# Gated mix of two attention branches: q and k weights loaded in column groups, heads at a stride of 32 floats in PSUM, later small loads, another order of all work

## The chip, the cores and the metric

One core of a Trainium2 chip. The metric is the time of one execution on the device in microseconds (us). Five in-order queues carry the program: PE (matrix multiplies, with its weight loads shown as PEld), ACT, DVE and POOL (elementwise engines), and SP, which here issues nearly all DMAs.

## The reference

The input x is 2048 tokens of 640 values. Both branches have 32 heads of 20 values, and a sigmoid gate per token mixes them.

```python
g = sigmoid((x * gate_w).sum(-1))
# branch A: linear attention, per head, feature map of 2 x 20
phi(q) = [softmax(q @ w_phi), softmax(-q @ w_phi)]        # and phi(k) alike
a = (phi(q) @ (phi(k).T @ v)) / (phi(q) @ phi(k).sum(0)) @ wo_A
# branch B: four segments of 512 tokens, per head
p     = softmax(q @ k.T * scale + causal_mask)            # inside the segment
a_dot = p @ v
a_mem = (elu1(q) @ M) / (elu1(q) @ z)                     # M, z from the segments before
o     = sigmoid(beta) * a_mem + (1 - sigmoid(beta)) * a_dot
M    += elu1(k).T @ v;   z += elu1(k).sum(0)
b = o @ wo_B
out = g * a + (1 - g) * b
```

## The kernel before

Everything is bfloat16 in on-chip memory with float32 sums in PSUM. Channels lie on partitions in five chunks of 128 (NCH = 5). For branch B, four heads share a chunk at offsets of 32 partitions: heads 0 to 19 take 20 of each 32 (the main part, 400 columns of the weights), and the 240 columns of the other 12 heads fill the 12 rows left in each block (the spare part). The weights of q and k are first loaded as they are (tiles stq and stk) and then copied into this image, WB, main and spare part apart (L606 and L607, called WB copies).

The work of branch B runs over four segments and, in each, eight groups of heads: matmuls of q with k (L754, called QK here) into PSUM, exp on ACT (L763, tiles expT, and ej for two of the groups), the causal mask on POOL (L767), and the product with the values v1B (L795, called PV), whose result oU is written to DRAM (opk) and read back as rows by head (oP) and as the row sums (dc). The reciprocals of the sums (L820) go out through rxB and come back spread over the rows (rrB), and L835 multiplies. b_mem accumulates M over the segments (L716, L719, and the masked product Mz, L721), b_out makes the memory part (Nmm on PE, then L864 to L869 into mo) and transposes it by DMA (moT).

Branch A makes the keys' features (E, with the norm at L909 on DVE or POOL), adds them up over all tokens, closes the sums with one column-sum matmul over all token tiles (a_fin, L962, called the column sum here), and then, per segment, makes the queries' features ET (L1008), their normalizer (rx, rr, L1040), the product U with the key-value sums (L1055), the reciprocal of the denominators (L1060) and the scaled result oA (L1064), which a DMA transposes (oTA). The last step (final, L1083 and L1084) multiplies oTA and oP by the output weights and adds both in PSUM; one copy to out and one DMA per token tile ends it.

The program builds one list of operations with dependencies. What runs where and when is written out: ORDER lists all operations in base 36 in the order in which they are given to their queues, CHOICE says for each eviction of PSUM whether ACT or DVE does it (L606 is the ACT form, L607 the DVE form, of the helper evac) and for each norm of E whether DVE or POOL does it, and WHERE names the buffer of each tile. An engine never passes a waiting instruction. spin is a matmul with no use, which keeps PE busy in the first microseconds.

Of the kernel before, what the change touches and what calls it, by code (L numbers as in the profile page):

```python
# [7 lines left out]
ALU = mybir.AluOpType  # L8
# [5 lines left out]
D = 640  # L14
H = 32
# [19 lines left out]
2t 3y 2r 3z 40 15 6v 34 7p 7w 3e 21 28 7x 22 23 35 3f 2w 26 27 2x 7q 29 24 2a 7m 6w 41 42 3g 25 43 7r 7n 45 2b 44 6y 2g 2h 30 4d 46 4f 32 4e 2c 2d 33  # L35
4g p3 p4 31 3h p5 p8 2 p9 6x c 49 4b 3i of e og 4a 3k 3j 2y 6z 2z 1r 3l on 3n 3m 2k oh 70 oo ok 39 op 1s oy 1t 2i 3o 3p 2l 2j 37 72 17 36 7i 2e 4h 1f
4c oz 2f 38 7j 47 4l pa 7k 16 4m 3b 48 4n 4o 3d 7l os ov ow 4p ox ot 4r ou 4i dc 4j 3c ol 4q 4s 8q dd 3a om p6 p7 4u 4v 4t oi pq 4w 4x pr ps 19 oq p0
oj 54 4y p1 55 or p2 80 50 ph 56 51 52 r4 81 4z 57 f 58 7u pe pi r5 pj pg 5c 53 59 pf 7v 7y 5d 5e 5l 5m 5n pk pl 10o 5a pb 7z 5g pc 85 pd 83 pv 5i 5o
3q 8a 18 5h 5v 8u 8b 8c 5f 5x qh 10p 5r 1u 73 pm qi 5w pn 74 4k dk 5s dl 5j 5k 5p 5t 6m 6n pw q1 q6 8t 6o q7 q8 5b q2 10q 5u 5y 5z 60 5q 61 6c 6e da
10r 6d po 67 di pp 71 68 84 db py c0 bw px 6f bz 69 63 dj pz 6p q0 pt 6a 6b 82 6q qb 64 r1 65 pu q3 qc 6i q4 6k r2 by qe q5 qs 75 76 6j bx 6l qf qg q9  # L40
dq qj qd 6r qa r3 8w c1 77 8d 66 8x 8y 88 dr dg qk 6s 8e 8f ql dh 90 91 92 c2 qt c4 do dp qu 1o 93 qm qo 6g 95 6h 96 94 97 ds qn 86 qp qv dt qw c3 qr
8z 9f 9g qq 98 8g qx sk qy 9h c5 c6 8h 9i 8i 9b r6 9c r9 9d 1e 87 rk 3 qz ho ra r0 sl rh sm hq r7 8j rb ri rj 8r rp 9j 8v rl 9e 89 8k 8l rm 99 6t rq
hr 9k r8 8s rr 9n 9o rs 9p 9l de rt df hp 9a rn hs s3 9w e2 9x rc 9y dm e3 ro e4 9r rd sf j8 ru dn rv 9s sg re rf rw rg s4 s5 62 e5 9q 9t j9 dv ht a6
s6 hu e6 s0 s7 a7 3r a8 hw e7 1c rx a2 s1 s2 sp 9z a9 sn s8 a4 sc ry a3 rz dx 9u 9v aa sq s9 so a0 a5 sd 7a se a1 ae j6 af ab j7 an ag ap ao j2 9m ac
# [39 lines left out]
def d_mm(*ns):  # L84
    return sum(max(n / 2400.0 + 0.004, 0.034) for n in ns)
# [222 lines left out]

class GatedMix(Graph):
# [167 lines left out]
    def setup(self):  # L477
# [695 lines left out]
```

## Time and profile before

| what | value |
|---|---|
| time, median of 3 runs | 329.12 us (329.91, 327.7, 329.12) |
| profiled execution | 332.06 us |
| span in its trace | 330.3 us (1.76 us lie around it) |
| busy in the span | PE 289.1 us (88%), ACT 247.8 (75%), DVE 234.9 (71%), POOL 124.6 (38%) |
| instructions | PE 2883, DVE 392, ACT 324, POOL 136 |
| DMA | 37.38 MB, mean 113 GB/s |
| granted PE clock over the span | 0.948 of full |

Busy shares are means over stages that have different limits: a share of 88% can be one stage at 99% and another with holes. The profiled execution is 2.94 us above the median of the three runs, and all sums over rows are made against it.

### The profile page before, as it was taken

What the parts mean: (1) busy time and instruction counts of PE and PEld (TensorE: products, weight loads), DVE (VectorE), ACT (ScalarE), POOL (GpSimd) and SP (SyncE); (2) the same over time, 40 slices, a digit from 0 to 9 for tenths busy, and PEclk for the clock granted to TensorE, in tenths of its full rate; (3) what the DMA queues carried; (4) which work ended last, traced back from release to release, by engine and by line L of the source; (5) the groups of instructions that cost most, each with busy time, mean ns of one, the idle gap of its engine ahead of it and who ended that gap; (6) DMA issues with size and microseconds to landing.
All of it is one profiled execution on the core that took longest, in us unless ns stands there. A gap on an engine that the chain in (4) does not pass through costs nothing.

```text
span 330.3 us, 7013 instructions
## 1 busy us (share of the span) xinstructions
PE 289.1 (88%) x2883; PEld 149.0 (45%) x2883; DVE 234.9 (71%) x392; ACT 247.8 (75%) x324; POOL 124.6 (38%) x136
## 2 busy tenths in 40 slices
PE   1899999999999969998899869997999668879695
PEld 1345554544545535445354444433444223446443
DVE  1444696989989999999998577565823736868740
ACT  4458889799887969897998729999897996941002
POOL 3321418238476546739342211244332373430000
PEclk9999999999999999999999999999999955579979
DMA  6992675050541441601506556661192263897933
GB/s 188 286 207 48 175 97 128 2 128 2 91 36 37 97 63 15 182 2 30 170 17 197 158 84 158 144 152 35 32 189 43 69 210 63 217 204 182 182 86 119
DMA packets 72271, 37.38 MB, mean 113 GB/s; under 512 B 55184, under 2 KB 69168, under 8 KB 72240
## 3 DMA queue, kind: packets, MB, share of 16 engines
q1 hardware_dynamic: 71488, 36.08, 47.8%
q10 hardware_dynamic: 656, 0.82, 0.7%
q8 instruction: 23, 0.38, 0.5%
q0 software_dynamic: 96, 0.04, 0.2%
q14 instruction: 8, 0.07, 0.1%
HBM read 14.01 MB, written 12.10 MB: 79 GB/s over the span
## 4 chain that ended last, share of the span: by engine, by line
PE 41%; DVE 21%; DMA 16%; ACT 11%; SPq 7%; issue 3%; POOL 0%; DVEq 0%
PE ps L627 9%; PE ps L1083 9%; ACT expT L763 7%; PE ps L1003 5%; DVE acc L949 4%; SPq L472 4%; PE ps L754 4%; SPq L468 3%; PE ps L795 3%; DMA dc<-opk 3%; DVE z L907 3%; PE ps L894 2%; DMA opk<-oU 2%; PE ps L1084 2%; DMA rrB<-rxB 2%
## 5 line engine op out<-in xcount | busy, mean ns | idle before, releaser
L763 ACT ACTIVATE expT<-ps 128x1024 bf16<-128x1024 f32 x128 | 124.5, 1030 | 20.8 <-PE ps L754 19.8
L767 POOL TENSOR_SCALAR_AFFINE_SELECT expT<-expT 128x512 bf16<-128x512 bf16 x96 | 72.4, 761 | 120.5 <-ACT expT L763 108.5
L627 PE MATMUL ps<-xT,WB 128*128 128x512 bf16 x200 | 50.6, 390 | 1.9 <-DVE oU L607 1.0
L763 ACT ACTIVATE ej<-ps 128x1024 bf16<-128x1024 f32 x32 | 31.2, 1040 | 3.0 <-PE ps L754 2.9
L909 POOL TENSOR_TENSOR E<-E,z 128x1280 bf16<-128x1280 bf16 x11 | 28.0, 2548 | 10.4 <-DVE z L908 9.4
L767 POOL TENSOR_SCALAR_AFFINE_SELECT ej<-ej 128x1024 bf16<-128x1024 bf16 x16 | 19.2, 1197 | 31.2 <-ACT ej L763 31.2
L1083 PE MATMUL ps<-Wo,oTA 128*128 128x512 bf16 x80 | 24.8, 395 | 5.5 <-DVE oP L877 4.7
L754 PE MATMUL ps<-qkm 20*128 20x512 bf16 (+3 forms) x320 | 21.7, 322 | 8.5 <-DVE oU L607 2.0
L627 PEld LDWEIGHTS ps<-xT,WB 128*128 128x128 bf16 x200 | 17.9, 100 | 23.9 <-issue 4.9
L949 DVE TENSOR_TENSOR acc<-acc,E 64x1280 bf16<-64x1280 bf16 x31 | 27.8, 896 | 1.2 <-DMA acc<-acc 0.3
L795 PE MATMUL ps<-expT,v1B 128*21 128x384 bf16 (+2 forms) x384 | 26.1, 342 | 2.6 <-POOL ej L767 1.2
L1008 ACT ACTIVATE ET<-ps 128x512 bf16<-128x512 f32 x40 | 22.5, 637 | 7.1 <-PE ps L1003 6.7
L606 ACT ACTIVATE out<-ps 128x640 bf16<-128x640 f32 x9 | 6.2, 703 | 28.6 <-PE ps L1084 22.8
L607 DVE CAST oU<-ps 128x512 bf16<-128x512 f32 x26 | 17.7, 682 | 10.3 <-PE ps L795 10.2
L907 DVE TENSOR_REDUCE z<-E 128x64 f32<-128x1280 bf16 x16 | 23.6, 1476 | 1.5 <-ACT E L901 1.4
L649 PE MATMUL ps<-WvB,xT 128*128 128x512 bf16 x80 | 23.9, 381 | 0.6 <-DVE M L716 0.5
L901 ACT ACTIVATE E<-ps 128x640 bf16<-128x640 f32 x32 | 22.1, 706 | 3.0 <-PE ps L895 2.5
L894 PE MATMUL ps<-WvA,xT 128*128 128x512 bf16 x80 | 23.6, 380 | 0.9 <-DVE qkm L607 0.5
L1003 PE MATMUL ps<-xT,WqA 128*128 128x512 bf16 x100 | 23.7, 380 | 0.5 <-DVE oA L1064 0.5
L894 PE MATMUL ps<-WkA,xT 128*128 128x512 bf16 x80 | 23.4, 380 | 0.5 <-DVE KVZacc L937 0.5
L1083 PE MATMUL ps<-Wo,oP 128*128 128x512 bf16 x80 | 23.8, 383 | 0.0
L607 DVE CAST qkm<-ps 128x512 bf16<-128x512 f32 x24 | 16.2, 683 | 8.0 <-PE ps L627 7.9
(130 smaller groups left out, 549.4 us busy)
## 6 DMA issues: line engine op xcount, KB each, us to landing
opk<-oU SPq DMA_DIRECT2D x16, 256.0 KB
oP<-opk SPq DMA_DIRECT2D x4, 640.0 KB
rx<-rc SPq DMA_DIRECT2D x16, 160.0 KB
rr<-rx SPq DMA_DIRECT2D x4, 640.0 KB
out_dram<-out SPq DMA_DIRECT2D x16, 160.0 KB
scr<-qkm SPq DMA_DIRECT2D x16, 120.0 KB
qks<-scr SPq DMA_DIRECT2D x16, 120.0 KB
stq<-in_B_wq_dram ACTq DMA_DIRECT2D x1, 800.0 KB, 5.2
```

Source lines behind the costliest of these rows:

```text
L607: return e.tensor_copy(o(), i())
L627: r = e.matmul(self.pf(pt, 0, 0, LSEG), lhsT=self.WB[:, w, kc, 128 * c:128 * (c + 1)], rhs=xT[:, kc, LSEG * n:LSEG * (n + 1)], start=(kc = ...
L754: r = e.matmul(self.pf(pts[i // 2], i % 2, c0, N), lhsT=view(32 * i, 32 * i + DH, 1, 128 * j, 128 * (j + 1)), rhs=view(32 * i, 32 * i + DH ...
L763: self.op("act", d_act(1024), lambda e, p=p, o=o: e.activation(o(), self.pbanks(pts[p], 0, 2, 512), ACT.Exp, scale=scale), W=[(pts[p], 0), ...
L767: self.op("pool", d_pool(n_el), lambda e: e.affine_select(view(), view(), pattern=pat, compare_op=ALU.is_ge, fill=0.0, base=0, channel_mul ...
L795: r = e.matmul(self.ps[32 * i:32 * i + 21, 512 * ad.t[0] + 128 * j:512 * ad.t[0] + LSEG], lhsT=vt[:, j, h, :], rhs=src[:, i, c0:c0 + N], s ...
L894: e.matmul(self.pf(pt, 0, 0, 512), lhsT=l, rhs=W[:, kc, 0:512], start=(kc == 0), stop=(kc == 4))
L907: self.op("dve", 1.48, lambda e: e.tensor_reduce(z[:, :], Ev(), axis=AX.X, op=ALU.add), R=[(E, 0), (E, 1)], W=[(z, "*")], claim=[rz], pr=p ...
L909: self.op(("dve", "pool"), {"pool": d_pool(1280, 2), "dve": 1.56}, lambda e: e.tensor_tensor(Ev(), Ev(), rz[:, :].rearrange("p (h o) -> p ...
L949: self.op("dve", 0.9, lambda e, src=src: e.tensor_tensor(acc[lo:lo + 64, :], acc[lo:lo + 64, :], src(), ALU.add), R=[(self.Et[t], 0), (sel ...
L1003: r = e.matmul(self.pf(pt, 0, 0, LSEG), lhsT=self.WqA[:, kc, 128 * c:128 * (c + 1)], rhs=xT[:, kc, LSEG * S:LSEG * (S + 1)], start=(kc == ...
L1083: e.matmul(self.pf(pt, 0, 0, 512), lhsT=l, rhs=self.Wo[:, c, 0:512], start=(c == 0), stop=(c == 9))
```

## The change

The loads of B's q and k weights, one DMA each before (stq on ACT's queue, stk on SP's behind the third part of xtok), become eight DMAs on SP: for the column groups (0,2) and (2,5) of the chunks, q and k, main and spare part. The copies into WB go by group, and a projection waits for the copies of its own group alone. The three loads on POOL's queue (gw, beta, wphi) wait for the first group of k. In PSUM, the tiles of Nmm and U have a head every 32 floats (ph) where they had a head every 21 in two banks, so the reciprocal, the product of mo and that of oA are one instruction of 640 columns where they were two of 320. There are 17 spins where there were 5, and they read the identity only. ORDER, CHOICE and WHERE are new.

```diff
-NSPIN = 5
+NSPIN = 17
 ORDER = """
-5 6 4 0 8 1h 1g 11 1i 7 1 k m o 1j s i q 14 r 9 l d 12 13 1k j a p n 2u 1l h 2v 1m 2m 2n b 1n 2o 2p 2s g 3u v 6u 7s 7o 3v 3w 2q t u x 10 y w 3x z 7t
+0 1 106 107 108 109 17 10a 10b 5 s t 7 6 4 8 1n 9 c 1o d w a 1p b f 1u e j x u 10c 1m g q 10d 1t h 10e 10f v r 2w 30 1s 1r 11 1q 3c 3d 2x m 38 39 1w
...
-CHOICE = "000110011010001011111111100111010100111111010000110111110001101111110011011101000111111111011010000100111111001111001111100111110011010001010001111010111100001000"
+CHOICE = "1111100011000101110011111100000101001111101001011001110111100110101110010111111010011110101101101110100000110111001011110101011110110111011111000111100001111100000100"
...
+CGRP = ((0, 2), (2, NCH))
...
+    def ph(self, t, h0, n, e=21):
+        return self.ps[:, 512 * t.t[0] + 32 * h0:512 * t.t[0] + 32 * (h0 + n)].rearrange("p (h e) -> p h e", e=32)[:, :, 0:e]
...
-        stq = self.dma("act", self.stq[:, :, :], wsrc(ins["B_wq"]), W=[(self.stq, "*")], pr=-50, name="stq", issue=0.45, lat=6.2)
-        stk = self.dma("sp", self.stk[:, :, :], wsrc(ins["B_wk"]), W=[(self.stk, "*")], pr=-50, name="stk", issue=0.5, lat=5.0, after=ld[2:3])
...
+        for gi, (c0, c1) in enumerate(CGRP):
+            for w, (st, name) in enumerate(((self.stq, "B_wq"), (self.stk, "B_wk"))):
+                src = wsrc(ins[name])
+                for z, (a0, a1) in enumerate(((80 * c0, 80 * c1), (400 + 48 * c0, 400 + 48 * c1))):
+                    stk = self.dma("sp", st[:, :, a0:a1], src[:, :, a0:a1], W=[(st, (z, gi))], pr=-50 + gi, name="s" + "AB"[gi] + "ms"[z], issue=0.5, lat=5.0)
+                    if gi == 0:
+                        ska = stk
...
-                self.op("pe", d_mm(*[512] * 5), mm, R=[(self.WB, (w, z, k0)) for z in range(2) for k0 in (0, 2)] + self.xr(n), W=[(pt, 0), (qk, (w, c))], pr=pr, name="qkproj")
+                self.op("pe", d_mm(*[512] * 5), mm, R=[(self.WB, (w, z, int(c >= CGRP[0][1]), k0)) for z, k0 in ((0, 0), (0, 3), (1, 0))] + self.xr(n), W=[(pt, 0), (qk, (w, c))], pr=pr, name="qkproj")
...
-            for f in range(2):
-                self.op("dve", d_dve(320, 1, True), lambda e, f=f, pt=pt, sm=sm, t=t, oA=oA: e.scalar_tensor_tensor(
...
+            self.op("dve", d_dve(640, 1, True), lambda e, pt=pt, sm=sm, t=t, oA=oA: e.scalar_tensor_tensor(
+                out=oA[:, :].rearrange("p (h d) -> p h d", d=DH), in0=self.ph(pt, 0, H, 32)[:, :, 0:DH],
+                scalar=self.g[:, t:t + 1], in1=sm[:, :].rearrange("p (h o) -> p h o", o=1).to_broadcast([128, H, DH]), op0=ALU.mult, op1=ALU.mult),
...
-            return e.matmul(self.pf(pt, 0, 0, 512), lhsT=self.ident[:, :], rhs=self.xT[:, 0, 0:512], start=True, stop=True)
+            return e.matmul(self.pf(pt, 0, 0, 512), lhsT=self.ident[:, :], rhs=self.ident[:, :].rearrange("p (o c) -> p o c", o=1).to_broadcast([128, 4, 128]), start=True, stop=True)
```

Over the whole program DVE goes from 392 to 362 instructions, ACT from 324 to 327, POOL from 136 to 138, and SP issues 181 DMAs where it issued 174. Three places where the order differs:

SP's queue at the start, before. xtok is the first 512 tokens, xT the transposed input of segment 1, WvB the values' weights, wkT a transposed weight of branch A.

```order
L472 DMA xtok<-in_A_x_dram 128x640 x4
L472 DMA stk<-in_B_wk_dram 128x5x640
L468 DMA_TRANSPOSE xT<-in_A_x_dram 128x5x512
L472 DMA WvB<-in_B_wv_dram 128x5x640
L468 DMA_TRANSPOSE wkT<-in_A_wqkv_dram 128x5x640
L468 DMA_TRANSPOSE wqT<-in_A_wqkv_dram 128x5x640
```

The same place after:

```order
L478 DMA xtok<-in_A_x_dram 128x640 x4
L478 DMA stq<-in_B_wq_dram 128x5x160
L478 DMA stq<-in_B_wq_dram 128x5x96
L478 DMA stq<-in_B_wq_dram 128x5x240
L478 DMA stq<-in_B_wq_dram 128x5x144
L478 DMA stk<-in_B_wk_dram 128x5x160
L478 DMA stk<-in_B_wk_dram 128x5x96
L478 DMA stk<-in_B_wk_dram 128x5x144
L478 DMA stk<-in_B_wk_dram 128x5x240
L474 DMA_TRANSPOSE xT<-in_A_x_dram 128x5x512
L478 DMA WvB<-in_B_wv_dram 128x5x640
L474 DMA_TRANSPOSE wkT<-in_A_wqkv_dram 128x5x640
```

Eight smaller loads stand where one stood, and stq comes ahead of stk on the same queue; the transposes follow them in both.

ACT's queue around the second segment's ET, the first after the column sum, before (eg is the gate, pq the feature of the queries for the memory, qkm a projection):

```order
L606 ACTIVATE oU_212<-ps 128x512
L763 ACTIVATE expT_205<-ps 128x2x512 x2
L653 ACTIVATE eg<-ps 128x1
L606 ACTIVATE v1B_60<-ps 128x32x20
L732 ACTIVATE pq_199<-qkm_56 128x1024
L1008 ACTIVATE ET_224<-ps 128x512 x10
L763 ACTIVATE expT_229<-ps 128x2x512 x2
```

The same place after:

```order
L617 ACTIVATE v1B_60<-ps 128x32x20
L774 ACTIVATE expT_197<-ps 128x2x512 x2
L774 ACTIVATE expT_207<-ps 128x2x512 x2
L743 ACTIVATE pq_212<-qkm_56 128x1024
L743 ACTIVATE pq_212<-qkm_56 128x1536
L1016 ACTIVATE ET_217<-ps 128x512 x6
L774 ACTIVATE expT_227<-ps 128x2x512 x2
```

Two more exps and the second pq stand ahead of ET, and ET is split around exps.

SP's queue in the last segment, before (opk is the last PV result of the kernel, rxB the reciprocals going out, rrB coming back):

```order
L472 DMA rr_298<-rx 128x5x512
L468 DMA_TRANSPOSE oTA_325<-oA_312 128x5x128
L472 DMA opk<-oU_317 128x2x512
L468 DMA_TRANSPOSE oTA_330<-oA_315 128x5x128
L472 DMA dc_327<-opk 128x1x128
L468 DMA_TRANSPOSE moT_318<-mo_320 128x5x128
L472 DMA oP_334<-opk 128x1x2560
L472 DMA out_dram<-out_247 128x640
L472 DMA rxB<-dc_327 4x32x128
L468 DMA_TRANSPOSE moT_318<-mo_322 128x5x128
L468 DMA_TRANSPOSE moT_318<-mo_333 128x5x128
L472 DMA out_dram<-out_324 128x640
```

The next row there is the load of rrB. The same place after:

```order
L478 DMA rr_300<-rx 128x5x512
L474 DMA_TRANSPOSE oTA_329<-oA_311 128x5x128
L474 DMA_TRANSPOSE oTA_331<-oA_309 128x5x128
L474 DMA_TRANSPOSE oTA_333<-oA_314 128x5x128
L478 DMA opk<-oU_324 128x2x512
L474 DMA_TRANSPOSE moT_317<-mo_321 128x5x128
L478 DMA dc_326<-opk 128x1x128
L478 DMA oP_334<-opk 128x1x2560
L474 DMA_TRANSPOSE moT_317<-mo_319 128x5x128
L478 DMA rxB<-dc_326 4x32x128
L474 DMA_TRANSPOSE moT_317<-mo_328 128x5x128
L478 DMA out_dram<-out_247 128x640
```

Again the load of rrB is next. The last opk now stands behind three transposes of oA where it stood behind one, and between rxB and rrB there is one transpose where there were two.

## Rows read from the trace of the kernel before

**Rows 1.** Windows: stretch, length, busy by engine (count), granted clock, DMA share, GB/s.

```profile
core 0: us, PE busy (x) PEld busy (x) DVE busy (x) ACT busy (x) POOL busy (x), PEclk, DMA share, GB/s
17.00:60.00 43.00, 42.82 (x374) 21.89 (x373) 28.25 (x38) 35.48 (x49) 14.92 (x15) 1.00 0.62 125
60.00:174.00 114.00, 106.03 (x1106) 55.81 (x1104) 108.58 (x150) 99.29 (x132) 63.24 (x54) 1.00 0.30 63
...
200.00:260.00 60.00, 55.85 (x589) 26.55 (x590) 33.01 (x59) 54.58 (x71) 20.32 (x28) 1.00 0.42 93
260.00:294.00 34.00, 25.57 (x292) 11.61 (x285) 21.84 (x43) 29.05 (x33) 16.15 (x21) 0.55 0.67 169
```

**Rows 2.** Timeline of SP, the first 10 us: start, length, instruction.

```profile
0.81 1.85 SPq L472 DMA_DIRECT2D xtok<-in_A_x_dram  x4
6.28 0.39 SPq L472 DMA_DIRECT2D stk<-in_B_wk_dram  x1
6.72 4.50 SPq L468 DMA_TRANSPOSE xT<-in_A_x_dram  x1
```

**Rows 3.** Timeline of PE and its weight loads, 6 to 17 us; idle before in brackets.

```profile
7.09 2.29 PE L510 MATMUL ps<-ident,xtok 128*128 128x128 bf16 x20 [7.09 <-DMA xtok<-in_A_x_dram]
10.24 6.21 PE L627 MATMUL ps<-xT,WB 128*128 128x512 bf16 x20 [0.86 <-ACT xT L606]
...
13.21 0.15 PEld L627 LDWEIGHTS ps<-xT,WB 128*128 128x128 bf16 x1 [0.28 <-issue]
13.63 0.15 PEld L627 LDWEIGHTS ps<-xT,WB 128*128 128x128 bf16 x1 [0.28 <-issue]
13.93 2.03 PEld L627 LDWEIGHTS ps<-xT,WB 128*128 128x128 bf16 x10 [0.15 <-ACT WB L606]
```

**Rows 4.** Timeline of ACT, the first exp.

```profile
16.83 1.94 ACT L763 ACTIVATE expT<-ps 128x1024 bf16<-128x1024 f32 x2 [2.95 <-PE ps L754]
```

**Rows 5.** DMA rates: a window while xtok lands, one while rx is issued.

```profile
4.00:4.50 0.50, 1.00 1.07 399
...
181.00:182.00 1.00, 1.00 (x15) 0.43 (x12) 0.76 (x4) 1.00 (x2) 0.00 (x0) 1.00 1.21 293
```

**Rows 6.** Timeline of SP: four DMAs of 640 runs of 256 bytes each.

```profile
178.03 5.46 SPq L472 DMA_DIRECT2D rx<-rc  x4
```

**Rows 7.** Groups of DVE by line and form: count, busy us, mean ns, idle before.

```profile
L909 DVE TENSOR_TENSOR E<-E,z 128x1280 bf16<-128x1280 bf16 x5 | 7.9, 1584 | 0.1
L607 DVE CAST oU<-ps 128x512 bf16<-128x512 f32 x26 | 17.7, 682 | 10.3 <-PE ps L795 10.2
L607 DVE CAST v1B<-ps 128x640 bf16<-128x640 f32 x5 | 4.0, 803 | 0.9 <-ACT eg L653 0.9
L719 DVE TENSOR_TENSOR M<-M,ps 128x420 f32<-128x420 f32 x2 | 1.2, 591 | 0.1
L721 DVE TENSOR_TENSOR Mz<-M,Mm 128x756 bf16<-128x756 f32 x3 | 3.2, 1081 | 0.1
L835 DVE TENSOR_TENSOR oP<-oP,rrB 128x1536 bf16<-128x1536 bf16 x4 | 3.8, 951 | 1.2 <-DMA rrB<-rxB 1.2
L1064 DVE SCALAR_TENSOR_TENSOR oA<-ps,g,cs 128x320 bf16<-128x320 f32 x32 | 16.0, 538 | 1.5 <-DMA moT<-mo 1.2
```

**Rows 8.** Timeline of DVE and of ACT after the column sum.

```profile
190.79 1.79 DVE L1040 TENSOR_TENSOR ET<-ET,rr 128x1024 bf16<-128x1024 bf16 x2 [3.04 <-DMA rr<-rx]
...
197.50 5.69 ACT L1008 ACTIVATE ET<-ps 128x512 bf16<-128x512 f32 x10 [5.88 <-PE ps L1003]
```

**Rows 9.** The chain of waits, last 36 us: start, length, what.

```profile
295.39 4.29 DMA opk<-oU
...
308.50 2.62 DMA rrB<-rxB
```

**Rows 10.** Timeline of SP in the last segment, and PE's first final.

```profile
303.61 0.58 SPq L472 DMA_DIRECT2D rxB<-dc  x1
304.24 3.58 SPq L468 DMA_TRANSPOSE moT<-mo  x2
...
314.32 0.58 PE L1083 MATMUL ps<-Wo,oTA 128*128 128x512 bf16 x1 [3.07 <-DVE oP L877]
```

More of the change, by code (lines that the diff above doesn't have):

```diff
@@ L37 @@
[L37 to L44, printed above, removed]
@@ L492, in setup @@
         ld = [self.dma("sp", xk[:, tl, :], x2d[128 * tl:128 * (tl + 1), :], W=[(xk, tl)], pr=-60 + tl, name="xk", issue=0.4, lat=2.5 + 0.6 * tl) for tl in range(4)]
-        stq = self.dma("act", self.stq[:, :, :], wsrc(ins["B_wq"]), W=[(self.stq, "*")], pr=-50, name="stq", issue=0.45, lat=6.2)
-        stk = self.dma("sp", self.stk[:, :, :], wsrc(ins["B_wk"]), W=[(self.stk, "*")], pr=-50, name="stk", issue=0.5, lat=5.0, after=ld[2:3])
-        wvb = self.dma("sp", self.WvB[:, :, 0:D], wsrc(ins["B_wv"]), W=[(self.WvB, "w")], pr=-49, name="WvB", issue=0.5, lat=5.2, after=[stq])
-        wkt = self.dma("sp", self.wkT[:, :, :], wqkv[0:D, D:2 * D], W=[(self.wkT, "*")], pr=-48, transpose=True, name="wkT", issue=4.5, lat=2.5, after=[stk])
+        for gi, (c0, c1) in enumerate(CGRP):
[5 more added lines that the diff above has]
+                        ska = stk
+        wvb = self.dma("sp", self.WvB[:, :, 0:D], wsrc(ins["B_wv"]), W=[(self.WvB, "w")], pr=-49, name="WvB", issue=0.5, lat=5.2)
+        wkt = self.dma("sp", self.wkT[:, :, :], wqkv[0:D, D:2 * D], W=[(self.wkT, "*")], pr=-48, transpose=True, name="wkT", issue=4.5, lat=2.5)
         wva = self.dma("sp", self.WvA[:, :, :], wsrc(wqkv[:, 2 * D:3 * D]), W=[(self.WvA, "*")], pr=-47, name="WvA", issue=0.5, lat=4.8)
@@ L501, in setup @@
         self.dma("sp", self.wqT[:, :, :], wqkv[0:D, 0:D], W=[(self.wqT, "*")], pr=-15, transpose=True, name="wqT", issue=3.7, lat=2.1)
[L502 to L504 removed]
+        self.dma("pool", self.WvB[:, :, D:D + 1], ins["gate_w"].rearrange("(c p o) -> p c o", p=128, o=1), W=[(self.WvB, "g")], pr=-26, noncontig=True, name="gw", lat=7.5, after=[ska])
+        self.dma("pool", self.beta[:, :], ins["B_beta"].partition_broadcast(128), W=[(self.beta, "*")], pr=-24, noncontig=True, name="beta", lat=8, after=[ska])
+        self.dma("pool", self.wphi[:, :, :], ins["A_w_phi"].rearrange("h d f -> (h d) f").rearrange("(c p) f -> p c f", p=128), W=[(self.wphi, "*")], pr=-22, noncontig=True, name="wphi", lat=8, after=[ska])
         for tl in range(4):
@@ L857, in mm @@
                         b = c // 4
-                        e.matmul(self.pf(mp, b, 84 * (c % 4), 84), lhsT=l, rhs=Mz[:, 84 * c:84 * c + 84], start=(c % 4 == 0 and b == 0), stop=True, skip_group_check=True)
-                        r = e.matmul(self.pf(mp, 1, 21 * (h0 - 16), 21 * nh), lhsT=l, rhs=Mz[:, 420 + 21 * j0:420 + 21 * (j0 + nh)], start=(c == 0), stop=True,
-                                     skip_group_check=True)
+                        e.matmul(self.ph(mp, 4 * c, 4), lhsT=l, rhs=Mz[:, 84 * c:84 * c + 84], start=(c % 4 == 0 and b == 0), stop=True, skip_group_check=True)
@@ L1054, in mm @@
                     for (c, h0, h1, f) in self.FUSE:
[L1055 removed]
+                        r = e.matmul(self.ph(pt, h0, h1 - h0 + 1), lhsT=ET[:, c, s, 128 * tl:128 * (tl + 1)],
                                      rhs=K1[:, s, c, h0 - HB[c]:h1 + 1 - HB[c], :], start=f not in seen, stop=True, skip_group_check=True)
```

101 lines of the change are left out of this document (50 added, 51 removed).

## The prediction

> **What bounds the kernel now.** I read the program as a row of stages, because its busiest engine changes. The windows come first [rows 1]. From 17 to 60 us PE is busy 42.82 of 43 us: nothing else counts there. From 60 to 174 us DVE is busy 108.58 of 114, with PE at 106.03 and ACT at 99.29: DVE ends most waits, but only 8 us lie between the window and PE's work, and no edit to DVE can win more. From 200 to 260 ACT is busy 54.58 of 60, PE 55.85, DVE only 33.01. From 260 to 294 ACT is busy 29.05 of 34 while PE has the clock at 0.55, that is near the lower level.
>
> Next the timelines of the four places where queues stand still. At the start PE first works at 7.09, released by the landing of xtok, though SP issued all of xtok between 0.81 and 2.66 [rows 2, 3]; stq was loading beside it. Projections begin at 10.24; the weight loads at 13.21 and 13.63 are 0.42 us apart, while from 13.93 ten take 2.03, 0.20 each: the first stretch ran at half rate [rows 3]. The first exp starts at 16.83 [rows 4]. After the column sum, DVE waits 3.04 us for rr, and ACT stands 5.88 us before ET at 197.50 [rows 8]. In the last 36 us the chain of waits goes through the last opk (issued 295.39) and rrB (issued only at 308.50) [rows 9], although rxB left at 303.61; between them SP issued two transposes in 3.58 us [rows 10]. PE waits 3.07 us and starts the finals at 314.32.
>
> **The change, part by part.**
>
> *Head.* Before, stq's 819 KB (640 x 640 values of 2 bytes) share the DMAs with xtok. After, SP issues xtok alone first. In a window while xtok lands 399 GB/s move [rows 5], so its four parts (655 KB) take 1.7 us from the first bytes, which I put at 2.6; they land near 4.3, not 7.0. Behind it go 1.64 MB of q and k in 5120 short runs (8 DMAs of 640, of 192 to 480 bytes). The trace has no such load. At 399 GB/s it takes 4.1 us; by the four DMAs of rx, 2560 runs in 5.46 us [rows 6], 10.9. The window of 181 to 182 us, inside the issue of rx, moved 293 GB/s [rows 5]; as it is the nearest case of many short runs in flight I take that: 5.6 us, which lands the first group of q (20% of the bytes, in order of issue) at 5.4, all of q at 7.1, the first group of k at 8.2, all at 9.9. The copies of the first q group are about 1.7 us of ACT and DVE work beside the transposes of x (PE 2.29 us for those [rows 3]), so the first projection comes at about 7.2: 3.0 earlier. Ten of the spins now run ahead of x, without waiting for any DMA, so PE has been busy before its first projection; if that brings the higher clock at once, the stretch from 10.24 to 13.93 at 0.20 us in place of 0.42 gives back half, 1.8 us more. The other end is the short runs at the rate of rx: all of k lands at 15.2 and the lead is lost. Head: -3.0, from -5 to 0.
>
> The Trainium skill has a rule against this part, in "DMA: Bandwidth & Descriptors", section "Specifications": line rate needs at least 512 bytes per transfer, and below that the engine does a read-modify-write. The 1280-byte runs of before were above it and all those of after are below. By that page the short runs would go at about half of 399 GB/s as an estimate, 8.2 us, and the sum would be some 1 us smaller in its gain; the window with 293 GB/s speaks for a milder loss. No row here shows a load with such runs.
>
> What the lead meets: SP's eight issues at 0.39 each [rows 2] end at about 6, so the transposes of x stand where they stood (6.72). PE's work from 17 to 60 us is solid, and a lead of 3 moves it whole only if values (WvB) and branch A's weights, whose issue doesn't move, are not late; they were needed behind 24 us, so I let the lead stand. gw, beta and wphi wait on POOL's queue for the first k group (8.2 us); the masks queued behind them begin after the first exp, which comes no earlier than 14, so this costs nothing, and without that cover would cost the first masks' delay. Of the other spins each is one matmul of 0.2 us in a hole: nothing.
>
> *The stage from 60 to 174.* Counting DVE's list ahead of the column sum against the new one, with prices of [rows 7]: two norms of E go to POOL (2 x 1.58 = 3.2), four oU casts to ACT (4 x 0.68 = 2.7), three casts of qkm likewise (of the same size, 2.0), four accumulations of M (4 x 0.59 at most, 2.4) and two Mz (2.2) move behind it. Added are four v1B casts (3.2), one more of values and one of a weight of A (640 wide too, 1.6) and one normalization of oP (0.95 and a smaller part, some 1.6). Net -12.5 + 6.4 = -6.1 us of DVE. POOL has room for two norms (63.24 of 114 [rows 1]). ACT gets seven casts and gives four v1B and others, near zero. Since PE leaves only 8 us, and DVE was not the last in every part of the stage, I take two thirds: -4.0, from -6 to 0.
>
> *After the column sum.* ET and U need sums that go out and come back through DRAM. The order puts two more exps and the longer pq ahead of ET, about 3.5 us of ACT's work in the 5.88 us that it stood, and the hole shrinks by 2 to 5 us. Against it ACT gets behind the column sum what it lost before it or what moved: two oU, an exp, a pq, an out, a v1B and one more cast, 5.4 us by their durations, in a stage where ACT has 5.4 us free of 60 [rows 1]. I take 0, from -3 to +3. One 640-wide oA in place of two of 0.538 costs at least what a 640-wide cast costs, 0.80, and at most 1.08 [rows 7]; with the same for mo and the reciprocals there are 28 instructions and at most 5 us of DVE less. They lie where DVE is busy 33 of 60: nothing on the path, but for the U chain near 195, which is in the range just given. The clock at 260 to 294 stays a matter of the same exps: 0.
>
> *Tail.* rxB's write should be readable one DMA time later, and rrB's load took 2.62 [rows 9]; 303.61 + 2.62 = 306.2, where it was issued at 308.5 because of two transposes. With one transpose and one out between, rrB is bounded by the write and not by SP: -2.3. Against it the last opk stands behind three transposes of oA in place of one, at about 1.8 each by the pair that took 3.58 [rows 10]; if they come after the last PV, two more cost up to 3.6, and if their oA were ready early, nothing. As U's products of the last segment are issued well before the last PV I take a cost of 0.3: -2.0, from -4 (finals at the higher clock from their first matmul as well) to +1.
>
> **The sum.** -3.0 - 4.0 + 0 - 2.0 = -9.0 from the profiled 332.06: 323.1. It stands 2.94 above the median, and I take the same distance: 320.1. The four half-widths, 2.5, 3, 3 and 2.5, taken as independent, give 5.5: a band of its own from 314.6 to 325.6.
>
> **The rivals.**
>
> *Only the ends pay.* In the long stage PE (106 of 114) and ACT (99) are nearly as full as DVE, and an engine relieved may only wait more. For it: the small idle left on PE. Against it: DVE's share of 95%. Head and tail alone: -5.0, 324.1.
>
> *All of it pays.* The warm clock gives the head 5, the stage 6, the hole 3, the tail 2: -16, 313.1. For it: each idle time is in the rows. Against it: it needs four good ends together.
>
> *The loads hold SP back.* If each of the eight DMAs of 640 runs keeps SP as one of rx's four did (5.46 / 4 = 1.37), the transposes of x start at 2.66 + 10.9 = 13.6, 6.9 later than 6.72 [rows 2, 6]. Head +4 in place of -3, the rest as forecast: -2.0, 327.1, no change. For it: the same number of runs of a like size. Against it: rx was written to DRAM, and its issue also waited on its source.
>
> *Slower: work moved behind the column sum.* ACT takes 5.4 us more where it is at 91% [rows 1]; if the hole is not filled, all of it is on the path. With 1 us of the head left, none of the stage and +0.5 in the tail: +4.9, 334.0. It decides from the point where the gain of head, stage and tail together is under 5.4 us. For it: ACT's share; against it: 5.88 us of idle at the very place, which the new order addresses.
>
> **Chances.** Forecast 0.46; only the ends 0.19; all of it 0.13; SP held back 0.10; slower 0.12. The first three are faster by over 1% (3.3 us, about what a measurement of this kernel can tell from no change) but for some 0.06 of the forecast's and the first rival's upper ends; those and the fourth give no change 0.16. Faster 0.72, same 0.16, slower 0.12. The range leaves out the slower case and half of the best one, 0.19 together, and reaches over the held-back case: 313 to 328.5.
>
> **What would show it.** In the profile after: xtok's transposes on PE near 4.5; weight loads of the first projections 0.2 apart; first exp near 14; x's transpose issued before 7 (after 10: held back). The column sum some 7 us earlier than before, with DVE no more over 90% throughout the stage. ACT's idle before ET under 4 us. rrB issued under 3 us behind rxB. Wrong would make it: WvB or wkT late behind 20 us; ACT over 95% from the column sum to the last PV; the last opk late behind its transposes.

## The result and the profile after

The changed kernel takes 315.9 us (median of 4 runs, 315.16 to 316.18), the kernel before 329.18 in the same comparison: a ratio of 0.9599, interval 0.9562 to 0.9636. The profiled execution is 315.9 us with a span of 314.2, against 332.06 and 330.3. Forecast was 320.1, with a range of 313 to 328.5. So 13.3 us were won by the medians and 16.1 between the two traces; the profiled execution of before lay 2.9 above its median, that of after on its median, and this distance, which the forecast kept, is 2.9 of the difference. Some executions of a kernel run in a slower state; the ratios and intervals here leave them out and the medians do not, so it is the ratios that are compared.

The windows of the kernel after, with the columns of [rows 1] (the column sum is at 165.1 where it was at 178.5):

```profile
17.00:60.00 43.00, 40.33 (x376) 20.99 (x384) 33.31 (x47) 33.52 (x47) 17.90 (x17) 1.00 0.56 115
60.00:165.10 105.10, 101.75 (x1053) 53.96 (x1058) 95.32 (x141) 96.72 (x129) 60.83 (x56) 1.00 0.31 71
...
200.00:250.00 50.00, 45.30 (x476) 22.87 (x480) 27.59 (x46) 44.24 (x58) 16.30 (x24) 1.00 0.45 106
250.00:284.00 34.00, 23.79 (x324) 11.70 (x322) 22.43 (x41) 30.83 (x35) 16.54 (x23) 0.75 0.69 181
```

The kernel before, cut at its own milestones (first exp about 17, column sum at 178.5, last exp begun at 290.9, first final of the last segment at 314.3):

```profile
0.00:17.00 17.00, 9.05 (x46) 4.64 (x47) 4.97 (x17) 7.04 (x10) 5.09 (x12) 1.00 0.89 232
...
60.00:178.50 118.50, 110.53 (x1160) 57.91 (x1159) 112.05 (x157) 103.58 (x137) 64.52 (x56) 1.00 0.31 65
178.50:290.90 112.40, 95.61 (x1021) 46.52 (x1021) 68.98 (x137) 94.64 (x120) 38.44 (x52) 0.88 0.53 129
290.90:314.30 23.40, 18.53 (x213) 11.37 (x211) 17.57 (x40) 4.35 (x7) 1.63 (x3) 0.94 0.84 182
314.30:330.30 16.00, 12.60 (x80) 6.71 (x80) 3.07 (x7) 2.71 (x4) 0.00 (x0) 0.90 0.34 95
```

and the kernel after, up to 60 us and behind the column sum:

```profile
0.00:15.20 15.20, 13.19 (x66) 6.50 (x68) 5.12 (x14) 7.99 (x15) 3.61 (x10) 1.00 0.96 200
15.20:60.00 44.80, 42.13 (x385) 21.67 (x393) 34.00 (x48) 35.32 (x49) 17.90 (x17) 1.00 0.58 125
...
165.10:280.90 115.80, 98.06 (x1097) 50.80 (x1100) 72.48 (x131) 101.49 (x130) 39.14 (x55) 0.91 0.54 140
280.90:300.10 19.20, 16.81 (x195) 10.81 (x199) 14.19 (x27) 4.95 (x8) 1.41 (x2) 1.00 0.84 177
300.10:314.20 14.10, 10.94 (x78) 6.10 (x80) 2.75 (x5) 2.00 (x3) 0.00 (x0) 0.97 0.50 118
```

Read stage by stage: from 60 us to the column sum 118.5 us became 105.1 (-13.4); from there to the last exp 112.4 became 115.8 (+3.4); the rest, 39.4, became 33.3 (-6.1). In the first stage DVE has 16.7 us less to do, PE 8.8, ACT 6.9; behind it ACT has 6.9 more and PE 2.5.

The timeline of SP's first issues, of PE, its weight loads and ACT in the kernel after ([rows 2 to 4] before):

```profile
2.67 2.49 SPq L478 DMA_DIRECT2D stq<-in_B_wq_dram  x4
5.20 3.21 SPq L478 DMA_DIRECT2D stk<-in_B_wk_dram  x4
8.45 3.80 SPq L474 DMA_TRANSPOSE xT<-in_A_x_dram  x1
...
12.92 6.87 SPq L474 DMA_TRANSPOSE wkT<-in_A_wqkv_dram  x1
...
4.02 1.81 PE L521 MATMUL ps<-ident,xtok 128*128 128x128 bf16 x15
...
7.71 6.64 PE L638 MATMUL ps<-xT,WB 128*128 128x512 bf16 x29 [0.47 <-ACT WB L617]
...
7.68 4.01 PEld L638 LDWEIGHTS ps<-xT,WB 128*128 128x128 bf16 x20 [0.93 <-DVE xT L618]
...
10.37 1.46 ACT L617 ACTIVATE WB<-stk 128x480 bf16<-128x480 bf16 x3 [1.46 <-DMA stk<-in_B_wk_dram]
...
15.09 1.97 ACT L774 ACTIVATE expT<-ps 128x1024 bf16<-128x1024 f32 x2
...
23.54 0.79 PE L604 MATMUL ps<-BD,wkT 128*128 128x140 bf16 x12 [1.07 <-DMA wkT<-in_A_wqkv_dram]
```

xtok is transposed by PE at 4.02 instead of 7.09, the first projection is 2.5 us earlier, weight loads are 0.20 us apart from its first one on, and the first exp is 1.7 earlier. But each of the eight loads held SP for 0.71 us on average (2.49 + 3.21 over 8), so x's transpose was issued at 8.45 and not before 7, wkT at 12.92 where it was issued at 11.90, and PE waits for wkT at 23.54.

Rows on the hole behind the column sum ([rows 8] before): DVE's wait for rr is 1.40 us instead of 3.04. ACT stands 2.63 us before one of the exps that are now listed ahead of ET and 0.92 in the middle of ET, 3.55 together, where it stood 5.88.

```profile
176.98 2.16 DVE L1048 TENSOR_TENSOR ET<-ET,rr 128x1536 bf16<-128x1536 bf16 x2 [1.40 <-DMA rr<-rx]
...
182.01 1.94 ACT L774 ACTIVATE expT<-ps 128x1024 bf16<-128x1024 f32 x2 [2.63 <-PE ps L765]
...
186.15 2.34 ACT L1016 ACTIVATE ET<-ps 128x512 bf16<-128x512 f32 x4
189.41 1.23 ACT L1016 ACTIVATE ET<-ps 128x512 bf16<-128x512 f32 x2 [0.92 <-PE ps L1011]
```

The chain of waits in the tail of the kernel after ([rows 9, 10] before):

```profile
284.05 4.08 DMA opk<-oU
...
291.94 2.46 DMA rxB<-dc
294.43 2.56 DMA rrB<-rxB
...
300.10 0.39 PE ps L1088
```

From the issue of the last opk to that of rrB it is 10.4 us (13.1 before); rrB follows rxB in 2.5 us (4.9 before); from the first final to the end 14.1 (16.0 before), with the clock at 0.97 of full where it was 0.90.

### The profile page after: what moved, and what is told of

Its sections match the earlier page's. It is cut to its first block, busy times and chain, and to the rows that moved or that the text cites. A ratio compares the mean times of both kernels' runs of the same rounds, so it can differ in the third digit from the quotient of the medians.

```text
span 314.2 us, 6978 instructions
## 1 busy us (share of the span) xinstructions
PE 282.9 (90%) x2856; PEld 149.8 (48%) x2895; DVE 223.9 (71%) x362; ACT 248.5 (79%) x328; POOL 122.9 (39%) x138
## 4 chain that ended last, share of the span: by engine, by line
PE 45%; DMA 18%; ACT 14%; DVE 9%; SPq 9%; issue 3%; POOL 1%; ACTq 0%; DVEq 0%
ACT expT L774 9%; PE ps L902 9%; PE ps L638 7%; PE ps L1088 6%; SPq L474 4%; SPq L478 4%; PE ps L1011 4%; PE ps L765 4%; DMA rr<-rx 4%; PE ps L806 3%; DMA wkT<-in_A_wqkv_dram 3%; PE ps L903 3%; ACT ej L774 2%; PE ps L1063 2%; PE ps L934 2%
## 5 line engine op out<-in xcount | busy, mean ns | idle before, releaser
L774 ACT ACTIVATE expT<-ps 128x1024 bf16<-128x1024 f32 x128 | 124.2, 1034 | 13.5 <-PE ps L765 13.4
L778 POOL TENSOR_SCALAR_AFFINE_SELECT expT<-expT 128x512 bf16<-128x512 bf16 x96 | 68.3, 719 | 116.4 <-ACT expT L774 114.7
L638 PE MATMUL ps<-xT,WB 128*128 128x512 bf16 x193 | 47.0, 380 | 1.8 <-issue 0.5
L917 POOL TENSOR_TENSOR E<-E,z 128x1280 bf16<-128x1280 bf16 x13 | 30.5, 2357 | 3.7 <-DVE z L916 3.7
L1011 PE MATMUL ps<-xT,WqA 128*128 128x512 bf16 x94 | 22.7, 380 | 0.7 <-issue 0.6
L1088 PE MATMUL ps<-Wo,oTA 128*128 128x512 bf16 x73 | 21.7, 379 | 1.0 <-DVE oP L885 1.0
L660 PE MATMUL ps<-WvB,xT 128*128 128x512 bf16 x74 | 22.3, 380 | 0.0
L902 PE MATMUL ps<-WvA,xT 128*128 128x512 bf16 x75 | 22.2, 380 | 0.0
L902 PE MATMUL ps<-WkA,xT 128*128 128x512 bf16 x74 | 21.7, 379 | 0.0
L1063 PE MATMUL ps<-K,ET 128*128 128x147 bf16 (+1 forms) x192 | 15.1, 244 | 5.8 <-DVE ET L1048 3.2
L618 DVE CAST qkm<-ps 128x512 bf16<-128x512 f32 x22 | 15.0, 683 | 7.0 <-PE ps L638 6.9
```

Source lines behind the costliest of these rows:

```text
L638: r = e.matmul(self.pf(pt, 0, 0, LSEG), lhsT=self.WB[:, w, kc, 128 * c:128 * (c + 1)], rhs=xT[:, kc, LSEG * n:LSEG * (n + 1)], start=(kc = ...
L660: e.matmul(self.pf(pt, 0, 0, 512), lhsT=l, rhs=self.WvB[:, kc, 0:512], start=(kc == 0), stop=(kc == 4))
L774: self.op("act", d_act(1024), lambda e, p=p, o=o: e.activation(o(), self.pbanks(pts[p], 0, 2, 512), ACT.Exp, scale=scale), W=[(pts[p], 0), ...
L778: self.op("pool", d_pool(n_el), lambda e: e.affine_select(view(), view(), pattern=pat, compare_op=ALU.is_ge, fill=0.0, base=0, channel_mul ...
L902: e.matmul(self.pf(pt, 0, 0, 512), lhsT=l, rhs=W[:, kc, 0:512], start=(kc == 0), stop=(kc == 4))
L917: self.op(("dve", "pool"), {"pool": d_pool(1280, 2), "dve": 1.56}, lambda e: e.tensor_tensor(Ev(), Ev(), rz[:, :].rearrange("p (h o) -> p ...
```

## The experiments

The theory that I set out to test: the gain is a shorter DVE list in the stage that DVE bounds, plus the tail, and the loads give a lead. The rival: the code edits (loads, merged products, spins) carry it. A third came out of the first results: the order and the assignment work only together. They ran on several chips, on which the kernel before took 330.8 to 331.8 us, so ratios to it are compared; the changed kernel has 0.9599.

**Merging alone, in the old order.** The two products of 320 become one of 640 (and the tiles get the stride of 32); nothing else.

```diff
-            for f in range(2):
-                self.op("dve", d_dve(320, 1, True), lambda e, f=f, pt=pt, sm=sm, t=t, oA=oA: e.scalar_tensor_tensor(
+            self.op("dve", d_dve(640, 1, True), lambda e, pt=pt, sm=sm, t=t, oA=oA: e.scalar_tensor_tensor(
...
```

> The kernel before in its own order, with the one-instruction products of mo and oA (28 DVE instructions fewer) and nothing else of the change. If merging is off the path, as the prediction's sum has it: 329 us, within 1.5. Rival: the products near the hole after the column sum and in the tail are on the path, each pair saving 0.1 to 0.27 us: 4 to 5 us less DVE there, and 325 or below.

332.35 us against 330.84, ratio 1.0057 (1.0004 to 1.0109): no gain. The 28 instructions lie off the path of this order.

**The tail's step alone, in the old order.** SP's list, with the load of rrB moved ahead:

```diff
-128 L468 DMA_TRANSPOSE moT_318<-mo_333 128x5x128
-129 L472 DMA out_dram<-out_324 128x640
-130 L472 DMA rrB_340<-rxB 128x1x512
+128 L472 DMA rrB_338<-rxB 128x1x512
+129 L468 DMA_TRANSPOSE moT_318<-mo_333 128x5x128
+130 L472 DMA out_dram<-out_324 128x640
```

> The kernel before with one thing changed: in the last segment the load of rrB is issued behind one transpose of mo after rxB, and not behind two and an out. The prediction's step: rrB 2.3 us earlier and the end with it, 327. Rival: the transpose that is now behind rrB comes late in its turn and the finals start as before: 329.

331.67 us, ratio 1.0033 (0.9983 to 1.0084): no gain. Its chain of waits shows why:

```profile
305.81 3.43 DMA rxB<-dc
309.26 2.63 DMA rrB<-rxB
311.92 0.97 DVE oP L835
313.06 0.58 SPq L472
313.68 2.63 DMA oTA<-oA
316.35 0.39 PE ps L1083
```

rrB now follows rxB in 3.45 us where it took 4.9, as meant, but the finals begin with the landing of an oTA whose transpose stands behind the transposes and outs that were pushed back. (In this execution rxB left 2.2 us later than before, so the comparison is of the distances.) The step is real, and in this order the next DMA of the same queue takes its place.

**The assignment alone, in the old order.** Evictions and norms go to the engines of the changed kernel.

```diff
-CHOICE = "000110011010001011111111100111010100111111010000110111110001101111110011011101000111111111011010000100111111001111001111100111110011010001010001111010111100001000"
+CHOICE = "000110011010110011111100000101001111101001011001110111100110101110010111111010011110101101101110100000110111001011110101011110110111011111000111100001111100000100"
```

> The kernel before in its own order and code, with the changed kernel's assignment of evictions to ACT or DVE and of norms to DVE or POOL. If the gain of the stage up to the column sum is DVE's shorter list (some 6 us less), this alone gives 4 to 6: 323 to 325. Rival: the assignment only pays in the order made for it; in the old order the evictions moved wait on a full ACT: 329 to 333.

367.41 us, ratio 1.1148 (1.1039 to 1.1257): 11% or 38 us slower, far past the rival. The work of the engines hardly changes (ACT is busy 250.0 us, DVE 234.2), their waits do: ACT's exps wait 38.2 us for QK on PE where they waited 19.8, DVE's oU casts 27.0 us for PV where they waited 10.2. That the evictions moved stand behind whatever the old order put into their new queues is the likely reason; it was not followed further.

**Order and assignment alone.** The changed kernel with the loads of before, two-instruction products, and without the spins ahead of x (the copies into WB by group stay):

```diff
-NSPIN = 17
+NSPIN = 7
...
+        stq = self.dma("act", self.stq[:, :, :], wsrc(ins["B_wq"]), W=[(self.stq, "*")], pr=-50, name="stq", issue=0.45, lat=6.2)
+        stk = self.dma("sp", self.stk[:, :, :], wsrc(ins["B_wk"]), W=[(self.stk, "*")], pr=-50, name="stk", issue=0.5, lat=5.0, after=ld[2:3])
...
+            for f in range(2):
+                self.op("dve", d_dve(320, 1, True), lambda e, f=f, pt=pt, sm=sm, t=t, oA=oA: e.scalar_tensor_tensor(
...
```

> The changed kernel's order and assignment, with the code edits undone: whole loads of stq on ACT's queue and of stk on SP as before, two-instruction products, no spins ahead of x. If the terms add up (head about 2, merging 0): 318. If the merged products or the loads carry the gain that the prediction did not see: 321 or more.

314.88 us, ratio 0.9558 (0.9457 to 0.966): the whole gain, better than either expectation, and the column sum comes when it does in the changed kernel:

```profile
L968 PE MATMUL ps<-onec,acc x10: 160/160/173, 165.1 to 165.3; 64*128 64x1 bf16 x10
```

None of these three code edits is needed for the gain; the order, its buffers and the assignment carry it.

The same edits undone one at a time:

```diff
 # new_unmerged: the products of before
+            for f in range(2):
+                self.op("dve", d_dve(320, 1, True), lambda e, f=f, pt=pt, sm=sm, t=t, oA=oA: e.scalar_tensor_tensor(
...
 # new_oldloads: two whole loads in place of the eight
+        stq = self.dma("act", self.stq[:, :, :], wsrc(ins["B_wq"]), W=[(self.stq, "*")], pr=-50, name="stq", issue=0.45, lat=6.2)
...
 # new_nospin: no spins at the start
-NSPIN = 17
+NSPIN = 7
```

> The changed kernel with the products of mo and oA in two instructions at a stride of 21, as before. If merging is off the path: 316, within 1. Rival: the new order is tight enough that 28 more instructions (at most 5 us of DVE) come through: 318 to 320.

> The changed kernel with stq whole on ACT's queue and stk whole on SP behind the third part of xtok, all copies waiting for the whole load. If the head's lead of the first exp (1.7 us) lasts to the end: 317.6, more if ACT and DVE wait longer for stk in the new order (up to 319). Rival: PE's waits later in the first segment take the lead up: 316.

> The changed kernel without the ten spins at the start. If the spins are what put the first projections at the higher clock: their weight loads are 0.4 us apart until PE has been busy for some time, and the first exp comes 1 to 2 us later: 317 to 318. Rival: the transposes of x warm PE as well as the spins do: 316.

315.75 (ratio 0.9587, 0.9509 to 0.9665), 316.54 (0.9619, 0.9533 to 0.9706) and 316.0 us (0.96, 0.9512 to 0.9689): none differs from the changed kernel's 0.9599, though the intervals, some 3 us to either side, could hide 1 to 2 us. The column sums are a finer measure: 165.8, 165.5 and 165.2 us, against 165.1. With the whole loads the first exp comes 2.0 us later. Without the spins the first projections do run at half the rate, and the first exp comes 2.0 us later too. The timelines of the run without spins, weight loads and ACT:

```profile
8.23 0.15 PEld L638 LDWEIGHTS ps<-xT,WB 128*128 128x128 bf16 x1 [0.28 <-issue]
8.66 0.15 PEld L638 LDWEIGHTS ps<-xT,WB 128*128 128x128 bf16 x1 [0.28 <-issue]
...
17.07 1.93 ACT L774 ACTIVATE expT<-ps 128x1024 bf16<-128x1024 f32 x2
```

So one half of the expectation holds (the spins bring the higher rate), the other (that it shows in the time) does not. That the two rates are two levels of the clock is not shown: the granted clock in the profile reads 1.00 in this stretch with the spins and without. The column-sum matmul of the changed kernel, by its line: duration, then first and last start.

```profile
L970 PE MATMUL ps<-onec,acc x10: 160/160/174, 165.1 to 165.3; 64*128 64x1 bf16 x10
```

The same line of the run without spins:

```profile
L970 PE MATMUL ps<-onec,acc x10: 160/160/174, 165.2 to 165.4; 64*128 64x1 bf16 x10
```

The 2 us are gone. The waits of PE between 15 and 60 us in the changed kernel say where:

```profile
PE ps L604 <- DMA wkT<-in_A_wqkv_dram: 1.1, 1, 1.1
PE ps L765 <- DMA qks<-scr: 0.9, 1, 0.9
```

Together 2.0 us; the run without spins has no wait of PE on a DMA in that stretch. PE that starts earlier meets the transposed weights and the re-read queries, which SP brings at the same time in both.

**The old assignment in the new order.**

```diff
-CHOICE = "1111100011000101110011111100000101001111101001011001110111100110101110010111111010011110101101101110100000110111001011110101011110110111011111000111100001111100000100"
+CHOICE = "1111100011000101001011111111100111010100111111010000110111110001101111110011011101000111111111011010000100111111001111001111100111110011010001010001111010111100001000"
```

> The changed kernel in its order with the assignment of evictions and norms of before. If DVE's shorter list is what shortened the stage up to the column sum by 8 to 10 us: 322 or more. Rival: the order did it and the assignment is worth little: 316 to 318.

359.31 us, ratio 1.0779 (1.0572 to 1.0985). It agrees with "322 or more" in sign only: against the changed kernel's 0.9599 the loss is 12%, some 39 us and nearly three times the whole gain, so this run does not measure what DVE's list is worth. It says the same as the assignment alone: neither of the two works without the other.

**Halves of the order.** Up to the column sum the one kernel's order, assignment and buffers, behind it the other's (a few buffers at the seam had to differ). The first with the loads, products and spins of before, the second on the code of before.

```diff
 # first_new: ORDER up to L962 from the changed kernel, then that of before
+0 1 11 5 m n 7 6 4 8 9 1h 1i q 1j 1o d r o 1g a k 1n b p l 2q 2u 1m 1l v 1k 36 37 2r g 32 33 1q 2s j c h 1r 2t s 2v t 2w i
...
 # second_new: ORDER up to L962 from before, then that of the changed kernel
+5 6 4 0 8 1h 1g 11 1i 7 1 k m o 1j s i q 14 r 9 l d 12 13 1k j a p n 2u 1l h 2v 1m 2m 2n b 1n 2o 2p 2s g 3u v 6u 7s 7o 3v 3w
...
```

> The changed order and assignment up to the column sum, with the loads, products and spins of before, and behind it the order and assignment of before. If the stages add up, the column sum comes 13 us earlier and what follows takes as long as before: 317. Rival: work was only pushed behind the column sum (5 us of PE, 5 of ACT), and what is left there in the old order has no place for it: 321 to 323.

> The order and assignment of before up to the column sum, the changed ones behind it, code of before. If the stages add up: the column sum at 178.5, and the later tail gain alone, 325 to 328. Rival: the second half only pays after the changed first half: 329 or more.

325.97 us, ratio 0.9836 (0.9775 to 0.9896), and 336.72, ratio 1.0157 (1.0099 to 1.0215). The column sum of the first comes at 166.1, of the second at 179.2: that half is kept. But the first gives most of it back behind the column sum. Its ACT waits there between 166 and 200 us:

```profile
ACT qkm L612 <- PE ps L633: 7.1, 2, 5.2
ACT eg L659 <- PE ps L656: 3.6, 2, 1.9
```

The projections and values that the new first half leaves undone have no place in the old second half; the last exp begins 3.3 us earlier than before, not 12. In the second, from 179 us on DVE waits 8.9 us for rr alone, in one piece. The stages do not add up; the rival of the first run (work was pushed behind the column sum) has the mechanism, with a larger price than its 321 to 323, and that of the second (329 or more) came true.

**DVE's list, shorter and longer.** In the old order the five norms of E on DVE do 4 of 64 groups and leave the others unnormalized; in the new order five row sums are done twice.

```diff
 # old_lessdve
+        nh = lambda e: 4 if e is self.nc.vector else 2 * H
...
-            Ev(), Ev(), rz[:, :].rearrange("p (h o) -> p h o", o=1).to_broadcast([128, 2 * H, DH]), ALU.mult),
+            Ev()[:, 0:nh(e), :], Ev()[:, 0:nh(e), :], rz[:, 0:nh(e)].rearrange("p (h o) -> p h o", o=1).to_broadcast([128, nh(e), DH]), ALU.mult),
 # new_moredve
-lambda e: e.tensor_reduce(z[:, :], Ev(), axis=AX.X, op=ALU.add)
+lambda e: [e.tensor_reduce(self.Mz[:, 64 * (t - 6):64 * (t - 5)], Ev(), axis=AX.X, op=ALU.add) if i else e.tensor_reduce(z[:, :], Ev(), axis=AX.X, op=ALU.add) for i in ((1, 0) if 6 <= t <= 10 else (0,))][-1]
```

> The kernel before, with the five norms of E that DVE does cut to 4 of their 64 groups (1.5 us down to some 0.1 each: about 7 us of DVE less; these tiles of E stay unnormalized). All five lie between 58 and 152 us. If DVE sets the pace of that stage, as the prediction has it: 4 to 7 us faster, 322 to 325 where before has 329 and the same below it on another chip. Rival: PE's and ACT's own lists set it (106 and 99 of 114 us), and the other engine's waits take it up: 0 to 2 us faster.

> The changed kernel with five row sums of E done twice on DVE between 60 and 160 us (1.48 us each, 7.4 us more; the second copy goes to a tile not yet in use). If DVE still sets the pace: 320 to 323. Rival: DVE's list is now the slack one there (95 of 105 us against PE's 102): 316 to 318.

325.74 us, ratio 0.9835 (0.9771 to 0.9898), and 323.06, ratio 0.9749 (0.9689 to 0.9808). DVE's groups by line, of the first:

```profile
L910 DVE TENSOR_TENSOR E<-E,z 128x80 bf16<-128x80 bf16 x5 | 1.8, 358 | 0.1
```

and of the second:

```profile
L915 DVE TENSOR_REDUCE Mz<-E 128x64 bf16<-128x1280 bf16 x5 | 7.4, 1475 | 0.0
```

In the first, DVE's list is 7.9 - 1.8 = 6.1 us shorter [rows 7] and the kernel 5.5 us faster (1.65% of 331.8). In the second it is 7.4 longer, and the kernel 5 us slower than the changed one by the ratios. So in either order a microsecond of DVE in that stretch costs 0.7 to 0.9 of one, with intervals of some 2 us around each of the two differences. The stage itself, from 60 us to the column sum, in the first and in the second:

```profile
60.00:175.30 115.30, 109.99 (x1157) 57.84 (x1155) 106.05 (x156) 103.21 (x137) 60.10 (x56) 1.00 0.30 68
...
60.00:174.90 114.90, 105.83 (x1077) 54.38 (x1073) 106.10 (x146) 97.64 (x130) 62.43 (x56) 0.99 0.28 65
```

In the new order DVE is busy 10.8 us more (the instructions around the added ones took longer too) and the stage is 9.8 longer: DVE sets the pace there. In the old order DVE is busy 6.0 us less and the stage only 3.2 shorter: about half of the relief is lost inside the stage, with PE busy 110.0 of 115.3 us and DVE waiting 3.3 us for PE ahead of KVZacc where it waited 1.8. That is the rival's mechanism at half its size. The rest of the gain shows only behind the column sum (the last exp begins 6.1 us earlier); why it shows there is open. In both runs the tile concerned is also ready at another time, so they price DVE's time in this stretch, not the length of its list alone.

## Why the prediction came out as it did

**The bound.** Right, with PE closer behind than one bound says. From 60 us to the column sum DVE's time counts in both orders; in the new one it sets the pace, in the old one about half of what DVE was relieved of was lost to waits inside the stage. The rival "only the ends pay" does not hold: the relief came through in the time, and the stage got shorter.

**The stage, forecast -4.0, range -6 to 0: the term that was mis-sized.** It measured -13.4. Three things were missed. First, the change of DVE's list up to the column sum, priced at -6.1 us. In the trace DVE was busy 145.3 us up to there before (4.97, 28.25 and 112.05 by stretches) and 134.4 after (5.12, 34.0 and 95.32): -10.8. Counted with the durations of before, the instructions that came and went make about -7, near my price; about 4 us more come from instructions that stand in both lists and took less time after. The six products pk are the largest item, before and after:

```profile
L698 DVE TENSOR_TENSOR pk<-pk,kT 128x1280 bf16<-128x1280 bf16 x6 | 7.0, 1166 | 0.1
...
L709 DVE TENSOR_TENSOR pk<-pk,kT 128x1280 bf16<-128x1280 bf16 x6 | 4.7, 802 | 0.0
```

No run shows why the same form takes another time. Second, I held the stretch up to 60 us to be PE's alone, where "nothing else counts". But DVE stood idle there for 14.75 of 43 us [rows 1], and up to 60 us the new order has it do 5.9 us more (33.2 to 39.1); three of the four v1B casts that I had added to the stage stand there. With both, DVE's work between 60 us and the column sum shrinks by 16.7 and the stage by 13.4. Third, PE did not cap it at 8, as I had argued from 106 of 114: PE's own list in the stage got 8.8 us shorter as well (110.53 to 101.75). By the counts of its weight loads 101 fewer stand in the stage, 42 more before 60 us (ten of them spins) and 79 more between the column sum and the last exp. A bound by another engine's busy time stands only while its list stays.

**The head, forecast -3.0.** The first projection came 2.5 us earlier, the first exp 1.7, and the higher rate was there from the first projection, as the run without spins shows by its lack. The step that failed is "I let the lead stand": PE meets wkT and qks 2.0 us early and waits, and wkT late behind 20 us is a sign of being wrong that the prediction names. Neither the whole loads nor the missing spins move the column sum by more than 0.4 us, nor do both together, so the head's share is 0 within what these runs can tell. The loads' rate: while they came in, windows of 1 us between 3 and 10 us show 203 to 276 GB/s (xtok and, from 8.45, x's transpose share them), and the first k group was copied at 10.37, 2.2 later than the 8.2 that I had by 293 GB/s. The rule of the Trainium skill in "DMA: Bandwidth & Descriptors", section "Specifications", on transfers under 512 bytes, points the right way here: the rate lies below the 293 taken and above the half that I worked out from it. By the prediction it would have cost some 1 us of the gain; with the lead lost anyway it cost nothing that these runs show.

**SP held back.** In part right: 0.71 us for each load, neither 0.39 nor 1.37; x's transposes 1.7 us later. wkT was issued 1.0 later, as much as PE's wait for it (1.07).

**Behind the column sum, forecast 0 of -3 to +3.** It measured +3.4, just past the range. The hole shrank by 2.3 us, the low end of the 2 to 5 counted (DVE waits 1.40 for rr, ACT stands 3.55 around ET), and ACT's list is 6.9 us longer where 5.4 was counted. So the moved work outweighs the hole. What it costs without the new second half is shown by the run with the new first half alone: some 9 of the 12 us won. The slower rival thus named a danger that was there; the new second half brought it down to 3.4, less than the stage won.

**The tail, forecast -2.0, range -4 to +1.** From the last exp to the end it measured -6.1, past the range; from the issue of the last opk on it took 34.9 us and takes 30.2: -4.8. The rrB step is there, -2.4 between rxB and rrB. The finals gave 1.9; their granted clock is higher (0.97 for 0.90), and what that alone is worth was not measured. The three transposes ahead of the last opk cost nothing: the last of them leaves SP at 284.01, when the last oU has just been copied (283.99), and the issue of opk follows the last exp by 3.2 us (4.5 before). But the run of the rrB step alone shows that this is no separate term: in the old order nothing came of it. Which moves won the rest of the tail is open.

**The merged products, forecast 0.** Right in both orders. One of 640 columns takes 0.870 for oA and 0.822 for mo, inside the bounds of 0.80 and 1.08:

```profile
L1069 DVE SCALAR_TENSOR_TENSOR oA<-ps,g,cs 128x640 bf16<-128x640 f32 x16 | 13.8, 870 | 0.3
...
L877 DVE TENSOR_TENSOR mo<-ps,cs 128x640 bf16<-128x640 f32 x12 | 9.8, 822 | 0.4
```

The sum came out within 4.2 us of the time, and 7.2 of the profiled execution (323.1 against 315.9). That this is not more is in part luck: a term of -4 was -13.4, one of -3 was 0, one of 0 was +3.4 and one of -2 was -6.1. The sum does not vouch for its parts. What stays open is which moves inside the order won the 5.9 us of DVE work ahead of 60 us, and what the choice of buffers has in it; no run moved them alone.

## What to carry to other kernels

With in-order queues and an order written out by hand, ask not only how much work the bounding engine loses in its stage, but how much of it can be done earlier, in a stage that another engine bounds and where it stands idle. A lead at the start of a kernel is worth nothing until one has followed the next operand of each engine that is led on; if it comes from a queue that didn't get faster, the lead ends there. Parts of a jointly made order (assignment, halves, one step) are not terms: tried alone, the assignment and the second half lost, the one step gave nothing, and the first half kept 5 of 13 us. A test of the bound itself, by adding or removing work, moved the time in the forecast direction in both orders, and the stage's own window then said which other engine was close behind.

## What the runs showed that was not expected

The size of the penalty for a mismatch: with 60 of the engine choices exchanged the kernel before takes 11% longer (ratio 1.1148), and the changed kernel 12% longer with the old choices (1.0779 against 0.9599). And the eight short-run loads hold SP 0.71 us each on average although nothing on SP waits for their data, where the whole load of before held it 0.39. The same DVE instruction on the same shape also differs between the two orders (pk 1.17 and 0.80 us), which no run explains.
